# Plain float32 attention products, value products by column halves, and the softmax division moved onto the output

## The chip, the cores and the metric

The kernel runs on one core of a Trainium2 chip. The metric is the device time of one execution in microseconds (us). The times of the kernel before are 739.14, 739.26 and 741.04 us, so the median is 739.26. The execution that the profiler recorded took 739.67 us; its span, from the first to the last instruction, is 737.8 us.

## The reference

A sparse attention (2 batches, 8 heads, 768 positions, head size 64) feeds two feed-forward blocks. All arrays are float32 except the weights of the feed-forward blocks, which come as float64.

```python
scores = scale * np.matmul(q, k.transpose(0, 1, 3, 2))
keep = is_global | is_local          # first 8 keys, or the last 96 positions
scores = np.where(keep, scores + bias, -1e9)
a = np.exp(scores - max); a = a / (sum(a) + 1e-9)
x = np.matmul(a, v)                  # then heads side by side: 1536 x 512
h = x @ w_in;  x = (h * tanh(softplus(h))) @ w_out                 # 512 -> 2048 -> 512
g = x @ w_gate; out = ((silu(g) * (x @ w_val)) @ w_out2)           # 512 -> 1536 -> 512
```

## The kernel before

**Tiles and steps.** Of each batch the 768 positions are 6 tiles of 128 rows. A tile's attention is done in two steps, each for four heads (two pairs, p; a pair holds heads j = 0 and 1): 24 steps s. Since a row looks at the first 32 keys and at most 96 positions back, a step needs the key block of its own tile and one more block, that of the tile before, whose first 32 rows are replaced by the first 32 keys of the batch (`move_k` and `move_v`, GpSimd). The first tile of a batch has one block only (4 of the 24 steps).

**One step.** `transp` (L415) turns q and k with four products with the identity into PSUM. `qk` (L466) computes the scores of four heads: the two heads of a pair lie on partitions 0 to 63 and 64 to 127, so each product uses 64 rows of the array. `softmax` adds the bias and takes the minimum (VectorE, L483), takes the exponential with its sum (ScalarE, L311), and scales the rows by 1/sum (GpSimd, L496). `pv` turns the scaled rows (L515), copies them out of PSUM, and multiplies them with v (L535); a product yields both heads of a pair for 128 x 256, half of which is not used, and two copies (`xs`) take the two used quarters out. GpSimd then writes the result into `x`.

**Products in parts.** All products but the transposes are in float32r. Where more precision is wanted, each operand is kept in two parts: the operand as float32r, and the rest that this leaves. Three passes (`PASSES`) are added up: first by first, first by rest, rest by first. So q and k, the turned rows `et`, v, the weights and the hidden values are each copied once and subtracted once.

**Feed-forward work.** 68 weight units are fetched as float64 and made into float32 by ScalarE (L380) and four VectorE operations (L913 to L916), and then split. The first 12 units serve the "A products": the first six column blocks of the first feed-forward block, in 18 jobs for 256 tokens each (L349 with 256 columns, 432 products, and L738, 432 products), which are mixed in between the attention steps. Two jobs share a `mish` with two changes of the ScalarE table (L687, L689). All other products (512 columns, L349) come after the attention, since their weights use its space.

**Order.** All operations are first listed with costs and priorities, and a planner (`Plan.order`) plays them through with its own costs and writes each engine's queue in the order that comes out. Each engine then works through its queue in that order; copies can go to more than one engine, and the planner chooses. Buffers are handed out in the order in which they were listed. The transposes and the value products share a pool of two PSUM banks, `t_p`: a step takes four buffers of it, one for the next tile's q and k, two for the turned rows, and one (`o`) for the value products. 56 products of zeros (L575, 512 columns) keep TensorE busy: 6 at the start, and 50 of the lowest priority where the planner finds TensorE with nothing else to do.

Of the kernel before, what the change touches and what calls it, by code (L numbers as in the profile page):

```python
# [204 lines left out]
def kernel(  # L205
# [183 lines left out]
    raws, vts, scs, ebs = {}, {}, {}, {}  # L389
# [13 lines left out]

    def transp(i, hf):
# [12 lines left out]
        pv = lambda: ps.t.rearrange("p (a b s) -> p a b s", a=2, b=2)  # L417
        view = lambda a: kq.t[:, a, prs, c:3:2 - c, :]
        keys = lambda a: [(kq, (a, c, hf)), (kq, (a, 2, hf))]
        pe(emit, [(xk, hf), (xq, hf)], [(ps, 0)], 4, 256)  # L420
        copy(lambda: view(0), pv, [(ps, 0)], keys(0), psum_in=True, on="AV")
        arith(lambda: view(1), pv, lambda: view(0).bitcast(F32), ALU.subtract, [(ps, 0)] + keys(0), keys(1), on="V")

    def move_k(i, hf):
        b, t = tiles[i]
        if t == NT - 1:
            return
        prs = slice(2 * hf, 2 * hf + 2)
        own = lambda: kq.t[:, :, prs, t % 2, 0:WG]
        g = lambda: kg.t[:, :, prs, :]  # L430
        keys = [(kq, (a, t % 2, hf)) for a in range(2)]
        if t == 0:
            copy(g, lambda: own().bitcast(F32), keys, [(kg, hf)], n=128, on="G")
        else:
            copy(own, lambda: g().bitcast(F32), [(kg, hf)], keys, n=128, on="G")

    def split_v(i):
        x = raws["v", i]
        vt = vts[i] = plan.buf(vt_p)
        raw = lambda: x.t.rearrange("p h d -> p (h d)")  # L440
        copy(lambda: vt.t[:, 0], raw, [(x, 0), (x, 1)], [(vt, 0)], on="G")
        arith(lambda: vt.t[:, 1], raw, lambda: vt.t[:, 0].bitcast(F32), ALU.subtract, [(x, 0), (x, 1), (vt, 0)], [(vt, 1)],
              on="G")

    def move_v(i):
        b, t = tiles[i]
        vt = vts[i]
        V = [(vt, 0), (vt, 1)]
        if t == 0:
            copy(lambda: vg.t, lambda: vt.t[0:WG].bitcast(F32), V, [(vg, 0)], n=1024, on="G")  # L450
        elif t < NT - 1:
            copy(lambda: vt.t[0:WG], lambda: vg.t.bitcast(F32), [(vg, 0)], V, n=1024, on="G")

    def qk(s):
# [701 lines left out]
```

## Time and profile before

| what | us |
|---|---|
| median of three runs | 739.26 |
| profiled execution | 739.67 |
| its span | 737.8 |
| TensorE busy | 692.3 (94%) |
| VectorE busy | 445.6 (60%) |
| ScalarE busy | 373.1 (51%) |
| GpSimd busy | 324.2 (44%) |

The shares are means over two very different parts. In the profile, PE is TensorE's products and PEld its weight loads, DVE is VectorE, ACT is ScalarE, POOL is GpSimd, SP issues the DMAs. L numbers are lines of the kernel. A busy share of a stretch says how full an engine was; what ended its idle time stands in the view of waits.

### The profile page before, as it was taken

Reading aid. Unit: us, or ns where it says so; the run is one execution under the profiler, and the core shown is the slowest. Engines: PE = TensorE matmul, PEld = TensorE weight load, DVE = VectorE, ACT = ScalarE, POOL = GpSimd, SP = SyncE. Lnnn points to the kernel's source line nnn. Section 1 sums busy time; section 2 is a strip of 40 time slices with the busy share of each in tenths; the row PEclk is TensorE's granted clock in tenths of the full one; section 3 lists DMA queues with packets and bytes.
Section 4 is the critical chain, followed back from the end, with each engine's and each line's share of the span. In section 5 each row is a group of like instructions: output and inputs, shape, how many; then the busy total and the mean of one; then the engine's idle time right before and its main releaser. Section 6 shows DMA issues by size and latency. Waiting matters only on the chain.

```text
span 737.8 us, 10293 instructions
## 1 busy us (share of the span) xinstructions
PE 692.3 (94%) x3761; PEld 579.2 (79%) x3761; DVE 445.6 (60%) x843; ACT 373.1 (51%) x676; POOL 324.2 (44%) x378
## 2 busy tenths in 40 slices
PE   8958889889889999998999999999999999999996
PEld 6647779879889987766887877788878888888885
DVE  6998998764767685897688799711184111211312
ACT  5768677874767878766777843221232211111111
POOL 4887888666445332584276455211232111111111
PEclk9999999999999999999999999999999999999999
DMA  7634444230004442352323323410030210300301
GB/s 178 163 103 115 115 129 137 65 76 11 30 2 127 148 155 87 115 157 74 113 87 114 100 73 116 141 58 0 1 127 16 84 32 2 115 0 1 114 1 61
DMA packets 73161, 61.55 MB, mean 83 GB/s; under 512 B 39824, under 2 KB 63376, under 8 KB 73104
## 3 DMA queue, kind: packets, MB, share of 16 engines
q1 hardware_dynamic: 73104, 60.83, 27.9%
q8 instruction: 31, 0.51, 0.3%
q14 instruction: 26, 0.21, 0.1%
HBM read 51.38 MB, written 9.44 MB: 82 GB/s over the span
## 4 chain that ended last, share of the span: by engine, by line
PE 57%; DVE 26%; ACT 8%; issue 5%; DMA 2%; POOL 1%; SPq 0%; DVEq 0%; ACTq 0%; POOLq 0%
PE bank L349 47%; DVE cv L915 4%; PE bank L738 4%; DVE cv L916 3%; DVE cv L913 3%; DVE cv L914 2%; PE bank L535 2%; DVE a L340 2%; DVE et L521 2%; DVE e L483 2%; DVE g L340 2%; PE bank L515 1%; DVE kq L340 1%; ACT u L311 1%; ACT cv L380 1%
## 5 line engine op out<-in xcount | busy, mean ns | idle before, releaser
L349 PE MATMUL bank<-x,wa 128*128 128x512 f32 (+1 forms) x1008 | 193.3, 345 | 2.6 <-DVE a L340 1.1
L349 PEld LDWEIGHTS bank<-x,wa 128*128 128x128 f32 x1008 | 161.2, 189 | 27.3 <-DVE a L340 1.8
L340 POOL TENSOR_TENSOR g<-a,g 128x512 fp32r<-128x512 f32 x55 | 76.5, 1391 | 222.1 <-ACT g L332 221.5
L349 PE MATMUL bank<-x,wb 128*128 128x512 f32 x648 | 157.5, 396 | 0.2 <-DVE a L340 0.2
L349 PEld LDWEIGHTS bank<-x,wb 128*128 128x128 f32 x648 | 121.9, 188 | 29.8 <-DVE a L340 0.7
L332 ACT ACTIVATE g<-a 128x512 fp32r<-128x512 f32 x64 | 40.2, 632 | 134.1 <-DVE a L708 115.1
L311 ACT ACTIVATE u<-bank 128x512 f32<-128x512 f32 x84 | 49.7, 592 | 89.4 <-PE bank L349 89.3
L706 DVE SCALAR_TENSOR_TENSOR a<-u,bank 128x512 f32<-128x512 f32 x36 | 24.7, 686 | 112.6 <-ACT u L311 112.6
L349 PE MATMUL bank<-g,wb 128*128 128x512 f32 x288 | 72.5, 403 | 4.2 <-DVE g L340 2.1
L349 PE MATMUL bank<-wa,g 128*128 128x512 f32 x288 | 70.9, 392 | 2.3 <-DVE sb L567 1.7
L349 PEld LDWEIGHTS bank<-g,wb 128*128 128x128 f32 x288 | 54.5, 191 | 19.7 <-DVE g L340 3.3
L708 DVE TENSOR_TENSOR a<-a,bank 128x512 f32<-128x512 f32 x36 | 24.7, 687 | 68.4 <-PE bank L349 68.3
L349 PEld LDWEIGHTS bank<-wa,g 128*128 128x128 f32 x288 | 53.6, 188 | 15.8 <-DVE sb L567 2.4
L496 POOL TENSOR_SCALAR e<-e,sm 128x256 f32<-128x256 f32 (+1 forms) x96 | 56.5, 603 | 15.3 <-DVE sm L492 13.5
L915 DVE SCALAR_TENSOR_TENSOR cv<-raw,cv 128x512 int32<-128x512 int32 x68 | 61.3, 904 | 1.2
L913 DVE TENSOR_SCALAR cv<-cv 128x512 f32<-128x512 f32 x68 | 39.2, 579 | 35.9 <-ACT cv L380 35.7
L916 DVE SCALAR_TENSOR_TENSOR cv<-raw,cv 128x512 int32<-128x512 int32 x68 | 59.2, 873 | 1.1
L535 PE MATMUL bank<-et,vt 128*128 128x256 f32 x264 | 45.2, 304 | 14.1 <-DVE et L521 13.9
L311 ACT ACTIVATE e<-e,mn 128x256 f32<-128x256 f32 (+1 forms) x96 | 46.2, 483 | 19.6 <-DVE mn L483 19.5
L738 PE MATMUL bank<-g,wa 128*128 128x256 f32 x432 | 55.6, 284 | 0.5 <-DVE g L340 0.5
L380 ACT ACTIVATE cv<-raw 128x512 f32<-128x512 f32 x68 | 44.8, 666 | 20.7 <-DMA raw<-in_moe_w_gate_dram 6.6
L738 PEld LDWEIGHTS bank<-g,wa 128*128 128x128 f32 x432 | 53.2, 191 | 0.8 <-DVE g L340 0.7
(103 smaller groups left out, 984.6 us busy)
## 6 DMA issues: line engine op xcount, KB each, us to landing
raw<-in_moe_w_out_dram SPq DMA_DIRECT2D x28, 512.0 KB, 3.4
raw<-in_moe_w_in_dram SPq DMA_DIRECT2D x16, 512.0 KB, 3.9
raw<-in_moe_w_gate_dram SPq DMA_DIRECT2D x12, 512.0 KB, 3.6
raw<-in_moe_w_val_dram SPq DMA_DIRECT2D x12, 512.0 KB, 3.6
part<-st SPq DMA_DIRECT2D x16, 256.0 KB, 2.4
sb<-part SPq DMA_DIRECT2D x12, 256.0 KB, 3.0
st<-part SPq DMA_DIRECT2D x12, 256.0 KB, 3.0
in_q<-in_q_dram SPq DMA_DIRECT2D x11, 256.0 KB, 3.2
```

The source lines that it names most:

```text
L311: nc.scalar.activation(out=o(), in_=i(), func=func, scale=scale, **args)
L332: lambda: nc.scalar.activation(out=o(), in_=i(), func=AF.Copy, scale=scale)),
L340: return lambda: eng.tensor_tensor(out=o(), in0=x(), in1=y(), op=alu)
L349: nc.tensor.matmul(out=o, lhsT=lhs(a), rhs=rhs(b), start=first and i == 0, stop=last and i == len(PASSES) - 1)
L380: op([("A", 520, lambda: nc.scalar.activation(out=wf(), in_=hi().bitcast(F32), func=AF.Abs))], R, W_)
L496: op([("G", 160 + 0.836 * n, lambda x=x, f=f: nc.gpsimd.tensor_scalar(out=x(), in0=x(), scalar1=f(), scalar2=1.0, op0=ALU.mult, op1=ALU.mu ...
L535: nc.tensor.matmul(out=o.t[:, p * 256:(p + 1) * 256], lhsT=vt.t[:, a, pr * P:(pr + 1) * P], rhs=et2[p].t[:, x, c].rearrange("p j s -> p (j ...
L706: dve(lambda: nc.vector.scalar_tensor_tensor(out=a.t, in0=u.t[:, 0], scalar=1.0, in1=hg.t, op0=ALU.add, op1=ALU.mult), U + [(hg, 0)], A_)
L738: nc.tensor.matmul(out=y.t[:, dl * SUB:(dl + 1) * SUB], lhsT=ws[fl].t[:, a, d * P:(d + 1) * P], rhs=g.t[:, b, fl * SUB:(fl + 1) * SUB], st ...
L913: lambda: ts(out=f(), in0=f(), scalar1=F64_LOW, scalar2=F64_HIGH, op0=ALU.max, op1=ALU.min),
L915: lambda: stt(out=w(), in0=high(), scalar=-0x40000000, in1=w(), op0=ALU.bitwise_and, op1=ALU.bitwise_or),
L916: lambda: stt(out=w(), in0=low(), scalar=29, in1=w(), op0=ALU.logical_shift_right, op1=ALU.bitwise_or),
```

## The change

The attention is computed in plain float32, with no parts: `kq`, `et` and v lose their second half, and with it the subtractions. A score or value product is one plain float32 product where three float32r passes stood. Value products are done per head: 64 columns of weights (that head's v), written to PSUM partitions 0 to 63 or 64 to 127, 128 columns each, so nothing unused is computed. The rows are no longer scaled by GpSimd: 1/sum of each head is spread over 64 partitions by a product of it (broadcast) with the identity, into the unused half of the bank `o`; it is copied out (`rs`) and multiplied into the output by one VectorE operation, which takes the place of the two `xs` copies. The block before is no longer patched by GpSimd but fetched a second time into a pool `u`, in two DMAs (32 and 96 rows). The products of zeros read another buffer.

```diff
-    kq = fixed(asb, [P, 2, NP, 3, P], F32R, "kq")
+    kq = fixed(asb, [P, NP, 3, P], F32, "kq")
-    raw_in = {n: Pool(slots(asb, 1 if n == "v" else 2, [P, H, D], F32, "in_" + n)) for n in "qkv"}
-    vt_p = Pool(slots(asb, 3, [P, 2, H * D], F32R, "vt"))
+    raw_in = {n: Pool(slots(asb, 2, [P, H, D], F32, "in_" + n)) for n in "qkvu"}
-    xs_p = Pool(slots(asb, 1, [P, 2, P], F32, "xs"))
-    et_p = Pool(slots(asb, 2, [P, 2, 2, 2, P], F32R, "et"))
+    xs_p = Pool(slots(asb, 2, [P, 2, P], F32, "xs"))
+    rs_p = Pool(slots(asb, 2, [P, 2 * P], F32, "rs"))
+    et_p = Pool(slots(asb, 2, [P, 2, 2, P], F32, "et"))
...
+    def load_previous(i):
+        b, t = tiles[i]
+        if t == 0:
+            raws["u", i] = raws["v", i]
+        elif t < NT - 1:
+            x = raws["u", i] = plan.buf(raw_in["u"])
+            for ks, k0, hk in ((slice(0, WG), 0, 0), (slice(WG, P), t * P + WG, 1)):
+                dma(lambda ks=ks, k0=k0: nc.sync.dma_start(
+                    out=x.t[ks], in_=v[b, :, k0:k0 + ks.stop - ks.start, :].rearrange("h s d -> s h d")), [],
+                    [(x, hk)], kb=2 * (ks.stop - ks.start))
...
-        arith(lambda: view(1), pv, lambda: view(0).bitcast(F32), ALU.subtract, [(ps, 0)] + keys(0), keys(1), on="V")
...
-                for n, (a, c) in enumerate(PASSES):
-                    for j in range(2):
-                        ro = slice(64 * j, 64 * j + 64)
-                        nc.tensor.matmul(out=banks[j].t[:, p * 256:p * 256 + nb * P], lhsT=kq.t[ro, a, pr, 2, :],
-                                         rhs=kq.t[ro, c, pr, 0:nb, :].rearrange("p b s -> p (b s)"), start=n == 0, stop=n == len(PASSES) - 1)
-        pe(emit, [(kq, (a, c, hf)) for a in range(2) for c in (2, 0, 1)[:nb + 1]], [(banks[0], 0), (banks[1], 0)], 12, 256)
+                for j in range(2):
+                    ro = slice(64 * j, 64 * j + 64)
+                    nc.tensor.matmul(out=banks[j].t[:, p * 256:p * 256 + nb * P], lhsT=kq.t[ro, pr, 2, :],
+                                     rhs=kq.t[ro, pr, 0:nb, :].rearrange("p b s -> p (b s)"), start=True, stop=True)
+        pe(emit, [(kq, (c, hf)) for c in (2, 0, 1)[:nb + 1]], [(banks[0], 0), (banks[1], 0)], 8, 256)
...
-            op([("G", 160 + 0.836 * n, lambda x=x, f=f: nc.gpsimd.tensor_scalar(
-                out=x(), in0=x(), scalar1=f(), scalar2=1.0, op0=ALU.mult, op1=ALU.mult))], [(sm, u)], [(e, u)])
...
-            dve(lambda et=et, pv4=pv4: nc.vector.tensor_tensor(
-                out=et.t[:, 1, 0:nb], in0=pv4()[:, 0:nb], in1=et.t[:, 0, 0:nb].bitcast(F32), op=ALU.subtract),
-                [(ps, 0), (et, 0)], [(et, 1)], n=n)
...
+        def over():
+            for u in range(4):
+                p, j = divmod(u, 2)
+                nc.tensor.matmul(out=o.t[64 * j:64 * j + 64, (2 + p) * P:(3 + p) * P],
+                                 lhsT=sm.t[:, u:u + 1].to_broadcast([P, D]), rhs=ident, start=True, stop=True)
+        pe(over, [(sm, u) for u in range(4)], [(o, 2)], 4, 256)
+        rs = plan.buf(rs_p)
+        copy(lambda: rs.t, lambda: o.t[:, 2 * P:4 * P], [(o, 2)], [(rs, 0)], n=256, psum_in=True, on="AV")
...
-                    for a, x in PASSES:
-                        nc.tensor.matmul(out=o.t[:, p * 256:(p + 1) * 256], lhsT=vt.t[:, a, pr * P:(pr + 1) * P],
-                                         rhs=et2[p].t[:, x, c].rearrange("p j s -> p (j s)"),
-                                         start=n == 0, stop=n == 3 * len(blks) - 1)
+                    for j in range(2):
+                        nc.tensor.matmul(out=o.t[64 * j:64 * j + 64, p * P:(p + 1) * P],
+                                         lhsT=v_of(c).t[:, 4 * hf + 2 * p + j, :], rhs=et2[p].t[:, c, j, :],
+                                         start=c == 0, stop=c == nb - 1)
...
-            copy(lambda ro=ro: xs.t[ro], lambda ro=ro, j=j: o4()[ro, :, j, :], [(o, 0), (o, 1)], [(xs, j)],
-                 psum_in=True, n=256, on="AV")
+        dve(lambda: nc.vector.tensor_tensor(out=xs.t.rearrange("p a s -> p (a s)"), in0=o.t[:, 0:2 * P],
+                                            in1=rs.t, op=ALU.mult), [(o, 0), (o, 1), (rs, 0)], [(xs, 0)],
+            n=256)
...
-                split_v(i)
+                load_previous(i)
...
-            if hh == 1:
-                move_v(ii)
```

Since the planner's operations and costs are others, every engine's queue is others too. Three places matter below.

First, TensorE in the middle of the attention, in the kernel before: the end of a step's scores (`kq`), then transposes of rows (`e`), value products (`vt`) and transposes of q and k.

```order
L466 MATMUL bank_102<-kq 128x256
L466 MATMUL bank_103<-kq 128x256
L515 MATMUL bank_104<-ident,e_129 128x128 x4
L535 MATMUL bank_105<-et_136,vt_124 128x256 x3
L535 MATMUL bank_105<-et_136,vt_125 128x256 x3
L535 MATMUL bank_105<-et_135,vt_124 128x256 x3
L535 MATMUL bank_105<-et_135,vt_125 128x256 x3
```

The same place in the changed kernel: value products of one step (L522), scores (L455), transposes (L499), a block of A products (L348) and the products that spread 1/sum (L511, from `sm`).

```order
L522 MATMUL bank_104<-et_137,in_v_122 64x128 x2
L522 MATMUL bank_104<-et_137,in_u_124 64x128 x2
L522 MATMUL bank_104<-et_138,in_v_122 64x128 x2
L522 MATMUL bank_104<-et_138,in_u_124 64x128 x2
L455 MATMUL bank_102<-kq 128x256
L455 MATMUL bank_103<-kq 128x256
L455 MATMUL bank_102<-kq 128x256
L455 MATMUL bank_103<-kq 128x256
L499 MATMUL bank_105<-ident,e_127 128x128 x4
L499 MATMUL bank_104<-ident,e_127 128x128 x4
L348 MATMUL bank_106<-x_73,wa_76 128x256 x12
L511 MATMUL bank_105<-ident,sm_130 64x128 x4
```

A step's 12 score products became 4, its 12 value products of 128 x 256 became 8 of 64 x 128, and 4 products for 1/sum came in, in a place of their own, ahead of the value products.

Second, VectorE in the second step of the kernel before, where the first weight unit (`cv`) comes in.

```order
L340 TENSOR_TENSOR kq<-bank_105,kq 128x2x2x128
L340 TENSOR_TENSOR kq<-bank_104,kq 128x2x256
L491 TENSOR_SCALAR sm_130<-sm_130 128x4
L492 RECIPROCAL sm_130<-sm_130 128x4
L913 TENSOR_SCALAR cv_91<-cv_91 128x512
L914 TENSOR_SCALAR cv_91<-cv_91 128x512
```

The first weight unit on VectorE in the changed kernel, which comes in the fifth step; `rs` is the spread 1/sum, L531 the multiplication.

```order
L328 TENSOR_SCALAR rs_136<-bank_104 128x256
L328 TENSOR_SCALAR kq<-bank_105 128x2x2x128
L531 TENSOR_TENSOR xs_134<-bank_104,rs_136 128x256
L480 TENSOR_SCALAR sm_132<-sm_132 128x4
L481 RECIPROCAL sm_132<-sm_132 128x4
L894 TENSOR_SCALAR cv_91<-cv_91 128x512
```

Weight units begin three steps later; in both kernels 16 of the 68 stand ahead of the end of the last step's bias work.

Third, TensorE at the end of the attention before: the last value products, the one transpose of the check of the arguments (L651), and A products behind them.

```order
L535 MATMUL bank_104<-et_135,vt_125 128x256 x3
L535 MATMUL bank_104<-et_135,vt_126 128x256 x3
L651 MATMUL bank_105<-ident,chk 1x128
L349 MATMUL bank_106<-x_75,wa_76 128x256 x12
L349 MATMUL bank_107<-x_75,wa_80 128x256 x12
```

And in the changed kernel:

```order
L522 MATMUL bank_104<-et_138,in_u_125 64x128 x2
L522 MATMUL bank_104<-et_138,in_v_123 64x128 x2
L635 MATMUL bank_105<-ident,chk 1x128
L348 MATMUL bank_104<-x_74,wa_80 128x256 x12
L348 MATMUL bank_105<-x_74,wa_84 128x256 x12
L348 MATMUL bank_104<-x_74,wa_82 128x256 x12
```

Of the 864 A products, 336 stand behind the last value products before, and 432 in the changed kernel. The 56 products of zeros, all ahead of the seventh step's scores before, are spread over the whole attention.

## Rows read from the trace of the kernel before

**Rows 1.** The profile's page: span, and engines' busy time with share and count.
```profile
span 737.8 us, 10293 instructions
PE 692.3 (94%) x3761; PEld 579.2 (79%) x3761; DVE 445.6 (60%) x843; ACT 373.1 (51%) x676; POOL 324.2 (44%) x378
```

**Rows 2.** Busy us by stretch (from:to length, engines with instructions, clock, DMA share).
```profile
0.00:120.00 120.00, 97.96 (x710) 83.63 (x711) 108.34 (x287) 84.70 (x224) 94.81 (x145) 0.97 0.50 127
120.00:212.00 92.00, 83.14 (x700) 76.91 (x700) 60.96 (x171) 62.84 (x142) 55.35 (x90) 1.00 0.22 59
212.00:260.00 48.00, 48.00 (x372) 46.58 (x370) 34.57 (x53) 35.66 (x46) 22.67 (x21) 1.00 0.37 117
260.00:738.00 478.00, 463.21 (x1985) 372.07 (x1983) 241.71 (x335) 189.89 (x267) 151.35 (x123) 0.99 0.23 74
```

**Rows 3.** Chain of waits, 0 to 120 us: shares by line, and its first transfer.
```profile
by line: DVE e L483 9.4%; DVE et L521 8.6%; DVE cv L916 8.2%; DVE cv L915 8.0%; issue 6.5%; DVE kq L340 5.3%; DVE cv L913 4.7%; DVE sm L491 4.5%; DVE wa L340 4.3%; PE bank L466 4.0%; PE bank L575 3.9%; PE bank L415 3.6%; ACT e L311 3.6%; PE
...
2.13 3.67 DMA in_k<-in_k_dram
```

**Rows 4.** Waits of TensorE, 0 to 212 us (waiter <- releaser: us, times, longest).
```profile
PE bank L535 <- DVE et L521: 13.9, 14, 2.3
PE bank L515 <- ACT xs L332: 4.9, 5, 1.9
PE bank L515 <- DVE xs L329: 2.3, 3, 1.2
```

**Rows 5.** Timeline of TensorE (start, us until its last end, what, count).
```profile
18.06 0.98 PE L466 MATMUL bank<-kq 64*128 64x256 f32 x12
18.96 0.44 PE L515 MATMUL bank<-ident,e 128*128 128x128 f32 x2
...
19.61 1.55 PE L575 MATMUL bank<-et 128*128 128x512 f32 x6
21.00 0.62 PE L535 MATMUL bank<-et,vt 128*128 128x256 f32 x3
21.46 0.28 PE L415 MATMUL bank<-ident,in_k 128*128 128x128 f32 x1
21.57 0.27 PE L415 MATMUL bank<-ident,in_q 128*128 128x128 f32 x1
...
211.32 0.86 PE L535 MATMUL bank<-et,vt 128*128 128x256 f32 x5 [0.34 <-DVE et L521]
...
230.84 5.32 PE L738 MATMUL bank<-g,wa 128*128 128x256 f32 x43
```

**Rows 6.** VectorE's groups by shape (count | busy us, mean ns | idle before).
```profile
L340 DVE TENSOR_TENSOR a<-bank,u 128x512 f32<-128x512 f32 x48 | 31.4, 683 | 8.9 <-ACT u L311 8.8
L521 DVE TENSOR_TENSOR et<-bank,et 128x512 fp32r<-128x512 f32 x40 | 26.7, 681 | 19.4 <-ACT et L332 19.3
L340 DVE TENSOR_TENSOR kq<-bank,kq 128x512 fp32r<-128x512 f32 x24 | 16.2, 680 | 3.5 <-ACT kq L332 3.3
L329 DVE TENSOR_SCALAR xs<-bank 64x256 f32<-64x256 f32 x11 | 4.6, 420 | 2.5 <-PE bank L535 2.4
L521 DVE TENSOR_TENSOR et<-bank,et 128x256 fp32r<-128x256 f32 x8 | 3.2, 415 | 0.1
```

**Rows 7.** ScalarE's groups by shape.
```profile
L311 ACT ACTIVATE u<-bank 128x512 f32<-128x512 f32 x84 | 49.7, 592 | 89.4 <-PE bank L349 89.3
L687 ACT ACT_TABLE_LOAD x24 | 30.8, 1283 | 0.4
L688 ACT ACTIVATE u<-u 128x1024 f32<-128x1024 f32 x24 | 25.5, 1061 | 0.3
L332 ACT ACTIVATE xs<-bank 64x256 f32<-64x256 f32 x37 | 14.0, 377 | 8.2 <-PE bank L535 7.0 <-DVE xs L329 0.7
L332 ACT ACTIVATE et<-bank 128x256 fp32r<-128x256 f32 x8 | 2.9, 381 | 1.1 <-PE bank L515 1.0 <-PE bank L535 0.2
```

**Rows 8.** GpSimd's groups by shape.
```profile
L496 POOL TENSOR_SCALAR e<-e,sm 128x256 f32<-128x256 f32 (+1 forms) x96 | 56.5, 603 | 15.3 <-DVE sm L492 13.5
```

More of the change, by code (lines that the diff above doesn't have):

```diff
@@ L388 @@
     NTL = len(tiles)
-    raws, vts, scs, ebs = {}, {}, {}, {}
+    raws, scs, ebs, sms = {}, {}, {}, {}
     def load(i, names="qk"):
@@ L415, in emit @@
                 nc.tensor.transpose(ps.t[:, p * P:(p + 1) * P], x.t[:, h:h + 2, :].rearrange("s h d -> s (h d)"), ident)
-        pv = lambda: ps.t.rearrange("p (a b s) -> p a b s", a=2, b=2)
-        view = lambda a: kq.t[:, a, prs, c:3:2 - c, :]
-        keys = lambda a: [(kq, (a, c, hf)), (kq, (a, 2, hf))]
         pe(emit, [(xk, hf), (xq, hf)], [(ps, 0)], 4, 256)
-        copy(lambda: view(0), pv, [(ps, 0)], keys(0), psum_in=True, on="AV")
-        arith(lambda: view(1), pv, lambda: view(0).bitcast(F32), ALU.subtract, [(ps, 0)] + keys(0), keys(1), on="V")
+        copy(lambda: kq.t[:, prs, c:3:2 - c, :], lambda: ps.t.rearrange("p (a b s) -> p a b s", a=2, b=2), [(ps, 0)],
+             [(kq, (c, hf)), (kq, (2, hf))], psum_in=True, on="AV")
     def move_k(i, hf):
@@ L428, in move_k @@
         prs = slice(2 * hf, 2 * hf + 2)
-        own = lambda: kq.t[:, :, prs, t % 2, 0:WG]
-        g = lambda: kg.t[:, :, prs, :]
-        keys = [(kq, (a, t % 2, hf)) for a in range(2)]
+        own = lambda: kq.t[:, prs, t % 2, 0:WG]
+        g = lambda: kg.t[:, prs, :]
         if t == 0:
-            copy(g, lambda: own().bitcast(F32), keys, [(kg, hf)], n=128, on="G")
+            copy(g, own, [(kq, (t % 2, hf))], [(kg, hf)], n=64, on="G")
         else:
[L435 to L452, printed above, removed]
+            copy(own, g, [(kg, hf)], [(kq, (t % 2, hf))], n=64, on="G")
     def qk(s):
@@ L476, in softmax @@
         e = ebs[s] = plan.buf(e_p)
-        sm = plan.buf(sm_p)
+        sm = sms[s] = plan.buf(sm_p)
         m = lambda u: mn.t[:, s * 4 + u:s * 4 + u + 1]
@@ L492, in softmax @@
         dve(lambda: nc.vector.reciprocal(out=sm.t, in_=sm.t), S4, S4, n=30)
-        for u in range(4):
-            x = lambda u=u: e.t[:, u, 0:n]
-            f = lambda u=u: sm.t[:, u:u + 1]
-            op([("G", 160 + 0.836 * n, lambda x=x, f=f: nc.gpsimd.tensor_scalar(
-                out=x(), in0=x(), scalar1=f(), scalar2=1.0, op0=ALU.mult, op1=ALU.mult))], [(sm, u)], [(e, u)])
     def pv(s):
@@ L501, in pv @@
         b, t = tiles[i]
-        e = ebs.pop(s)
+        e, sm = ebs.pop(s), sms.pop(s)
         blks = (0,) if t == 0 else (0, 1)
         nb = len(blks)
-        v_of = lambda c: vts[i if c == t % 2 else i - 1]
+        v_of = lambda c: raws["v", i] if c == t % 2 else raws["u", i - 1]
         et2 = []
@@ L544, in pv @@
         xs = plan.buf(xs_p)
-        for j in range(2):
-            ro = slice(64 * j, 64 * j + 64)
-            copy(lambda ro=ro: xs.t[ro], lambda ro=ro, j=j: o4()[ro, :, j, :], [(o, 0), (o, 1)], [(xs, j)],
-                 psum_in=True, n=256, on="AV")
+        dve(lambda: nc.vector.tensor_tensor(out=xs.t.rearrange("p a s -> p (a s)"), in0=o.t[:, 0:2 * P],
+                                            in1=rs.t, op=ALU.mult), [(o, 0), (o, 1), (rs, 0)], [(xs, 0)],
+            n=256)
         dst = lambda a: x.t[:, a, 2 * hf:2 * hf + 2, o0:o0 + P]
         ks = lambda a: [(x, (a, 2 * hf + p, o0 // P)) for p in range(2)]
-        XS = [(xs, 0), (xs, 1)]
-        copy(lambda: dst(0), lambda: xs.t, XS, ks(0), n=256, on="G")
-        arith(lambda: dst(1), lambda: xs.t, lambda: dst(0).bitcast(F32), ALU.subtract, XS + ks(0), ks(1), n=256,
+        copy(lambda: dst(0), lambda: xs.t, [(xs, 0)], ks(0), n=256, on="G")
+        arith(lambda: dst(1), lambda: xs.t, lambda: dst(0).bitcast(F32), ALU.subtract, [(xs, 0)] + ks(0), ks(1), n=256,
               on="G")
```

24 lines of the change are left out of this document (8 added, 16 removed).

## The prediction

> **What bounds the kernel now.** I read the page first: TensorE is busy for 94% of the span, the others for 44 to 60% [rows 1]. Then the stretches, since the mean hides two programs [rows 2]. From 212 us on TensorE is all but full (511 of 526 us): what happens there is the time of its products. Up to 120 us VectorE is the fullest engine (108.3 of 120 us, TensorE 98.0). The chain of waits up to 120 us confirms it [rows 3]: mostly VectorE, with the two operations that the change deletes in it, the subtraction for the rest of the rows (L521) at 8.6% and that of q and k (L340 on `kq`) at 5.3%. TensorE's waits up to 212 us say the same from its side [rows 4]: 13.9 us for L521, 7.2 us for the `xs` copies, which also go. So the attention stretch is bound by VectorE and ScalarE together, and the change takes work from them and gives work to TensorE. The question is whether TensorE has room for it.
>
> TensorE's room, from the timeline [rows 5]. The unit costs: a plain float32 transpose of 128 columns starts 0.11 us after the one before (21.46 to 21.57); a float32r product of 256 columns takes 0.12 (43 in 5.3 us); one of 512, 0.23 (six zero products between 19.61 and 21.00); the 12 score products of a step 0.90 (18.06 to 18.96). Two score products on the two halves of the rows run at the same time: 12 x 0.12 would be 1.44. Six pairs at 0.12 are 0.72, so 0.18 of the 0.90 goes into entering and leaving the split array. Over the attention stretch: 272 transposes at 0.11 are 29.9 us, 264 value products at 0.12 31.7, 24 steps of scores 21.6, 56 zero products 12.9, and the 528 A products ahead of the last value product (864 less 336) 63.4. The sum is 159.5 of 212 us. The first keys land only at 5.8 us [rows 3], so 46.5 us are left in which TensorE waits or is late.
>
> **The change part by part.**
>
> VectorE and ScalarE lose the rests, 26.7 + 3.2 us for the rows and 16.2 for q and k, and the `xs` copies, 4.6 + 14.0: 64.7 us [rows 6, 7]. They gain a copy of 128 x 256 out of PSUM per step (nearest row: 0.38 us on ScalarE [rows 7]) and a multiplication of that size (0.415 on VectorE [rows 6]): 24 x 0.80 = 19.1. In the new order 96 A products more stand behind the attention; they are two jobs with one `mish`: two reads of PSUM, two table changes and two long passes on ScalarE, 2 x 0.59 + 2 x 1.28 + 2 x 1.06 = 5.9 us [rows 7], and some 2.7 us on VectorE (two products at 0.68 [rows 6] and as much again for splitting). So of the 316.8 us that both engines are busy up to 212 us [rows 2], 262.6 are left.
>
> GpSimd loses the scaling of the rows, 56.5 us [rows 8], and the splitting and patching of v. It is not the fullest engine anywhere, but the scaling stands between 1/sum and the transposes, so each step also gets 4 x 0.60 us shorter.
>
> TensorE: no plain float32 product stands in this trace, only transposes. From below, such a product costs what one float32r pass costs, 0.06 us per 128 columns; from above, four passes, 0.24. The nearest row is the plain float32 transpose, 0.11 per 128 columns, about twice float32r: there one operand is an identity, which is exact in one part. A product has two full operands, so I take twice that, 0.22 per 128 columns, as two passes of 0.11, one after the other on their part of the array. The Trainium skill states four passes for true float32 (FP8 and Floating Point Precision, TensorE Precision Notes); by that the price would be the upper end, 0.24, and the sum would be 5 us longer.
>
> Whether two halves of the array still overlap is the second unknown. Rows on 64 and 64 partitions do with float32r [rows 5]; halves by columns do not occur in the trace. Bounds: full overlap, and none. I take overlap for both, since the nearest row shows it, but in the order written: both passes of one head, then both of the other, so that a pass can only start beside the second pass of its neighbour. Then n products take n + 1 slots of one pass and not 2n. To each group in halves I add the 0.18 from above.
> - Scores, 20 steps with two blocks: 5 slots of 0.22 + 0.18 = 1.28 instead of 0.90, together +7.6 us. The 4 steps with one block come out within 0.2 us of before.
> - Value products: 9 slots of 0.11 + 0.18 = 1.17 instead of 12 x 0.12 = 1.44, together -5.4.
> - Spreading 1/sum: new, 5 x 0.11 + 0.18 = 0.73, 24 times, +17.5.
> Together +19.7 us on TensorE. The Trainium skill gives the reason for the 0.18, and it speaks against the change: changing the tiling mode drains TensorE (TensorEngine Tiling (Array Packing), Key Properties). The change adds two such groups per step.
>
> Fetching the block before twice costs 16 DMAs on SP's queue. The DMA engines are busy for 50% up to 120 us and 22% after [rows 2], and weight units begin three steps later in the new order; I take nothing. If SP's queue stands at such a fetch because its buffer is still in use, weight fetches behind it come late; that would be about one landing per case, 3.7 us as for the first keys [rows 3], with A products that wait for the unit.
>
> **The sum.** Attention stretch after: 159.5 + 19.7 - 96 x 0.12 (the A products that move behind) = 167.6, and 6 at the start, so TensorE can't end it before 173.6 us. Of the 46.5 us of waiting I keep 15: of about 31 us that TensorE stands still up to 212 us (212 less 181.1 busy [rows 2]), 21.1 are for operations that go [rows 4], so a third stays (one multiplication takes the place of the two `xs` copies, on an engine that is no longer full). That is 188.6. VectorE and ScalarE then have 262.6 us of work in 2 x 188.6, 70% full, against 75% before and 80% up to 120 us: no longer the bound, though near it. What is late next is TensorE itself. The last value product ended at 212.2 [rows 5], 525.6 us before the end; to these come the 11.5 us of A products: 537.1. Span 725.7; the profiled execution has 1.9 us around its span, so 727.6, taken as 728. That execution is 0.4 us above the median, which changes nothing.
>
> **Rivals.**
>
> 1. The column halves do not overlap. For it: no row shows them overlapping. Against it: the row halves do. Value products then take 16 x 0.11 + 0.18 = 1.94 (+11 us with the one-block steps instead of -5.4), 1/sum 8 x 0.11 + 0.18 = 1.06 (25.4 instead of 17.5): 24.7 us more than in the forecast. TensorE needs 198 us; being fuller, it keeps only 10 of waiting: 208, a span of 745, 747 us. It decides as soon as TensorE's added work is more than the waiting that goes, 31.5 us (the A products that move shorten one stretch and lengthen the other). The Trainium skill is against this rival: it reports column packing as concurrent, 2.38 times faster for three tiles (TensorE: Matmul & The Clock Gate, Part 3); no run here shows it.
> 2. Plain float32 products overlap in no half. Scores 8 x 0.22 + 0.18 = 1.94, 14 us more: TensorE needs 212, with 10 of waiting 222, 761 us.
> 3. The waiting is not given back. `over` takes the bank `o` before the value products and holds it until the multiplication; the pool has two banks, so the next tile's transposes wait longer. Price: the 0.73 of the new group and about 0.2 for its hand-over, 24 times, 22 us, of which A products cover some 9: 728 + 13 = 741. For it: TensorE's waits on L515 for `xs` [rows 4] are waits for such a bank. Against it: the `et` copies and the scaling, which lengthened the same loop, are gone.
> 4. A plain product costs a single pass. Then 1/sum and value products are nearly free, TensorE's sum is some 25 us below before, and VectorE and ScalarE are the bound at 80%: 164 us and 6 at the start, 170 + 537 + 2 = 709.
>
> **Chances.** Forecast 0.50 (its own range 717 to 738, from 4 to 25 us of waiting kept), rival 1 0.22, rival 2 0.10, rival 3 0.13, rival 4 0.05. The range 714 to 757 leaves out most of rivals 2 and 4. A change of 0.3% (2.2 us) is about what can be told from none: faster takes 0.47 of the forecast, 0.04 of rival 3 and rival 4: 0.56; the same 0.02, 0.06 and 0.01 of rival 1: 0.09; slower the rest, 0.35.
>
> **What will show it.** In the changed profile: score groups (L455) of four take 1.1 to 1.3 us if row halves overlap, 1.8 to 2.0 if not; four products of 1/sum (L511) 0.55 to 0.75 or 0.9 to 1.1; eight value products (L522) 1.0 to 1.2 or 1.8 to 2.0. VectorE up to 120 us should fall well below 90%. The last value product should end near 189 us; near 208, rival 1. If L499 waits long for `xs` or `rs`, rival 3. The forecast is wrong if TensorE's groups cost more than 1.5 times these numbers, or if the stretch behind the last value product is not 537 us, since nothing in my sum touches it but the A products.

## The result, and the profile after

| | before | changed |
|---|---|---|
| median, us | 739.2 (4 runs, 738.67 to 741.04) | 719.52 (4 runs, 719.23 to 719.93) |
| profiled execution / its span, us | as above | 719.93 / 718.2 |
| last value product ends, us | 212.2 | 182.9 |
| from there to the end of the span, us | 525.6 | 535.3 |

The ratio is 0.9727 (95% interval 0.971 to 0.9743): the change makes the kernel 19.7 us faster. The forecast was 728 us, in a range of 714 to 757.

The span and the busy times on the profile's page of the changed kernel; they answer to [rows 1].

```profile
span 718.2 us, 10474 instructions
PE 692.5 (96%) x3945; PEld 566.8 (79%) x3945; DVE 400.7 (56%) x797; ACT 358.6 (50%) x648; POOL 238.6 (33%) x250
```

VectorE, ScalarE and GpSimd all have less work; TensorE has as many busy microseconds as before, in a shorter span. By stretch, with the columns of [rows 2] (the attention now ends at 183, not at 212):

```profile
0.00:120.00 120.00, 111.06 (x948) 83.21 (x948) 96.91 (x323) 87.81 (x249) 51.09 (x88) 1.00 0.68 159
120.00:183.00 63.00, 61.22 (x549) 53.97 (x549) 24.93 (x77) 33.37 (x76) 17.36 (x24) 1.00 0.18 51
```

Up to 120 us TensorE went from 97.96 to 111.06 us busy, VectorE from 108.34 to 96.91. From 120 us to the end of the attention TensorE is busy for 61.2 of 63 us. The granted clock there is at 1.00, where the mean of the first 120 us was 0.97 before.

The chain of waits of the changed kernel, 0 to 120 us, as shares by line; it answers to [rows 3]:

```profile
by line: PE bank L455 13.7%; PE bank L499 11.5%; PE bank L522 10.9%; PE bank L348 10.4%; PE bank L559 9.2%; PE bank L426 9.0%; PE bank L511 7.3%; DVE cv L894 3.2%; issue 3.1%; DMA in_k<-in_k_dram 3.0%; DVE cv L896 2.8%; DVE e L472 2.4%; DVE
```

The first seven entries are TensorE: scores, transposes, value products, A products, zeros, q and k, and the new spreading of 1/sum (L511). Before, VectorE's lines led. TensorE's longest waits up to 183 us, in the columns of [rows 4]:

```profile
PE bank L522 <- DVE rs L328: 2.2, 4, 0.6
PE bank L522 <- ACT rs L331: 1.9, 4, 0.5
PE bank L559 <- DVE g L556: 1.5, 1, 1.5
PE bank L426 <- DMA in_k<-in_k_dram: 1.0, 1, 1.0
PE bank L499 <- DVE xs L531: 0.9, 1, 0.9
```

The 13.9 us on the subtractions are gone, and of the 7.2 us on the `xs` copies 0.9 are left. What is new is small: 4.1 us in which the value products wait for the copy `rs` (L328 on VectorE, L331 on ScalarE), though by the kernel they only share the bank that it reads.

TensorE's timeline in the middle of the attention (start, us until its last end, what, count; a plain float32 product leaves two records, so x8 at L455 is four products):

```profile
59.92 0.66 PE L511 MATMUL bank<-ident,sm 128*64 128x128 f32 x8
60.51 0.33 PE L426 MATMUL bank<-ident,in_k 128*128 128x128 f32 x1
...
62.99 0.66 PE L499 MATMUL bank<-ident,e 128*128 128x128 f32 x4 [0.80 <-DVE kq L328]
63.58 1.13 PE L455 MATMUL bank<-kq 64*128 64x256 f32 x8
64.64 0.55 PE L499 MATMUL bank<-ident,e 128*128 128x128 f32 x3
...
181.83 0.44 PE L522 MATMUL bank<-et,in_u 128*64 128x128 f32 x4
182.10 0.39 PE L522 MATMUL bank<-et,in_v 128*64 128x128 f32 x4
182.31 0.39 PE L522 MATMUL bank<-et,in_u 128*64 128x128 f32 x4
182.53 0.39 PE L522 MATMUL bank<-et,in_v 128*64 128x128 f32 x4
182.85 0.27 PE L635 MATMUL bank<-ident,chk 128*1 128x128 f32 x1
```

From the start of a group to the start of the next: spread 0.59 us, scores 1.06, eight value products 1.02. All three are cheaper than forecast (0.73, 1.28, 1.17).

### The profile page after: what moved, and what is told of

It reads as the page before. It is cut to its first block, busy times and chain, and to the rows that moved or that the text cites. A ratio compares the mean times of both kernels' runs of the same rounds, so it can differ in the third digit from the quotient of the medians.

```text
span 718.2 us, 10474 instructions
## 1 busy us (share of the span) xinstructions
PE 692.5 (96%) x3945; PEld 566.8 (79%) x3945; DVE 400.7 (56%) x797; ACT 358.6 (50%) x648; POOL 238.6 (33%) x250
## 4 chain that ended last, share of the span: by engine, by line
PE 66%; DVE 16%; ACT 9%; issue 5%; DMA 2%; POOL 1%; SPq 0%; DVEq 0%; ACTq 0%; POOLq 0%
PE bank L348 48%; PE bank L722 5%; DVE cv L894 3%; PE bank L455 3%; DVE cv L896 3%; DVE cv L897 3%; PE bank L499 3%; PE bank L522 2%; ACT L671 2%; DVE cv L895 2%; DVE a L339 2%; PE bank L426 2%; PE bank L559 2%; ACT u L672 2%; PE bank L511 2%
## 5 line engine op out<-in xcount | busy, mean ns | idle before, releaser
L348 PE MATMUL bank<-x,wa 128*128 128x512 f32 (+1 forms) x1008 | 192.3, 345 | 1.5 <-POOL wa L339 0.6
L348 PEld LDWEIGHTS bank<-x,wa 128*128 128x128 f32 x1008 | 161.4, 189 | 26.6 <-issue 1.0
L339 POOL TENSOR_TENSOR g<-a,g 128x512 fp32r<-128x512 f32 x60 | 84.4, 1407 | 231.2 <-ACT g L331 229.5
L348 PE MATMUL bank<-x,wb 128*128 128x512 f32 x648 | 157.2, 395 | 1.3 <-DVE a L339 1.3
L348 PEld LDWEIGHTS bank<-x,wb 128*128 128x128 f32 x648 | 121.6, 188 | 30.7 <-DVE a L339 1.8
L331 ACT ACTIVATE g<-a 128x512 fp32r<-128x512 f32 x66 | 41.2, 631 | 131.7 <-DVE a L692 114.9
L348 PE MATMUL bank<-wa,g 128*128 128x512 f32 x288 | 70.9, 392 | 2.2 <-DVE st L551 1.8
L348 PE MATMUL bank<-g,wb 128*128 128x512 f32 x288 | 70.2, 397 | 2.4 <-POOL g L339 1.6
L348 PEld LDWEIGHTS bank<-g,wb 128*128 128x128 f32 x288 | 53.9, 188 | 16.7 <-POOL g L339 2.5
L348 PEld LDWEIGHTS bank<-wa,g 128*128 128x128 f32 x288 | 53.6, 188 | 15.8 <-DVE st L551 2.5
L897 DVE SCALAR_TENSOR_TENSOR cv<-raw,cv 128x512 int32<-128x512 int32 x68 | 57.6, 848 | 1.0
L896 DVE SCALAR_TENSOR_TENSOR cv<-raw,cv 128x512 int32<-128x512 int32 x68 | 57.3, 845 | 1.2
L339 POOL TENSOR_TENSOR wa<-cv,wa 128x512 fp32r<-128x512 f32 x27 | 35.4, 1310 | 54.0 <-ACT wa L331 51.9
L339 POOL TENSOR_TENSOR wb<-cv,wb 128x512 fp32r<-128x512 f32 x27 | 37.5, 1389 | 29.1 <-ACT wb L331 27.9
```

The lines of the kernel that those rows point to most:

```text
L331: lambda: nc.scalar.activation(out=o(), in_=i(), func=AF.Copy, scale=scale)),
L339: return lambda: eng.tensor_tensor(out=o(), in0=x(), in1=y(), op=alu)
L348: nc.tensor.matmul(out=o, lhsT=lhs(a), rhs=rhs(b), start=first and i == 0, stop=last and i == len(PASSES) - 1)
L896: lambda: stt(out=w(), in0=high(), scalar=-0x40000000, in1=w(), op0=ALU.bitwise_and, op1=ALU.bitwise_or),
L897: lambda: stt(out=w(), in0=low(), scalar=29, in1=w(), op0=ALU.logical_shift_right, op1=ALU.bitwise_or),
```

## The experiments

Theory A is the prediction's: the attention waits for VectorE and ScalarE; what is taken from them shortens it until TensorE is the bound. Theory B puts the gain on GpSimd: the scaling of the rows, which stood between 1/sum and the transposes, is gone. Theory C: TensorE's own products became cheaper. In the table "T" is the end of the last value product in the profiled execution; medians stand beside runs of the kernel before on the same chip.

| run | kernel | median, us | ratio to before (95%) | T, us |
|---|---|---|---|---|
| e1_scores | before + scores plain | 731.22 | 0.9899 (0.9859 to 0.9939) | 208.8 |
| e2_values | before + values plain | 725.38 | 0.9804 (0.9761 to 0.9848) | 195.2 |
| e3_nospread | changed, GpSimd scales rows | 712.42 | 0.964 (0.9605 to 0.9675) | 184.4 |
| e4_order | changed, halves one after the other | 720.68 | 0.975 (0.9714 to 0.9786) | 183.9 |
| e5_nozero | changed, 50 zero products out | 719.55 | 0.9709 (0.9677 to 0.9741) | 191.1 |
| e6_dvework | changed + 72 idle operations on VectorE | 731.72 | 0.9871 (0.9839 to 0.9903) | 204.4 |
| e7_merge | changed, spread joined to a value group | 726.93 | 0.9806 (0.9775 to 0.9837) | 183.4 |
| e8_plainzero | changed, zero products plain float32 | 726.48, one run | none | 176.3 |
| e9_double | changed, spread issued twice | 729.33 | 0.985 (0.9823 to 0.9878) | 191.6 |
| e10_nospread_nozero | e3 + e5 | 714.68 | 0.966 (0.9634 to 0.9686) | 184.8 |
| e11_changed | changed, again | 719.17 | 0.9711 (0.9687 to 0.9735) | 183.5 |

**Which part pays.** e1 takes the kernel before and makes only the scores plain.

```diff
-    kq = fixed(asb, [P, 2, NP, 3, P], F32R, "kq")
+    kq = fixed(asb, [P, NP, 3, P], F32, "kq")
...
-        arith(lambda: view(1), pv, lambda: view(0).bitcast(F32), ALU.subtract, [(ps, 0)] + keys(0), keys(1), on="V")
...
-                for n, (a, c) in enumerate(PASSES):
+                    nc.tensor.matmul(out=banks[j].t[:, p * 256:p * 256 + nb * P], lhsT=kq.t[ro, pr, 2, :],
```

> The kernel before with one part of the change alone: scores in plain float32 (q and k without rests). Theory A (VectorE and ScalarE bounded the attention, and taking their work away made the time): 24 subtractions of 0.68 us go (16.2 us), TensorE gets 20 x 0.16 = 3 us more; about half of 16 comes out: 731 us (727 to 735). Rival B (the scaling by GpSimd between 1/sum and the transposes was what each step waited for): scaling stays, so 739 (736 to 743). Rival C (TensorE's own products became cheaper): 742, the 3 us more.

Measured: 731.22, 7.6 us below before, as theory A had it. Theory C fails for this part: TensorE's score groups became dearer (1.06 us instead of 0.90), and the kernel faster. The wait on the other subtraction, which e1 keeps, is still TensorE's longest up to 212 us in e1:

```profile
PE bank L530 <- DVE et L516: 9.5, 14, 1.6
```

e2 makes only the value products plain, by column halves, and fetches the block before twice; GpSimd still scales the rows, and nothing is spread.

```diff
-    et_p = Pool(slots(asb, 2, [P, 2, 2, 2, P], F32R, "et"))
+    et_p = Pool(slots(asb, 2, [P, 2, 2, P], F32, "et"))
...
-                    for a, x in PASSES:
+                    for j in range(2):
+                        nc.tensor.matmul(out=o.t[64 * j:64 * j + 64, p * P:(p + 1) * P],
+                                         lhsT=v_of(c).t[:, 4 * hf + 2 * p + j, :], rhs=et2[p].t[:, c, j, :],
...
-        for j in range(2):
+        copy(lambda: xs.t.rearrange("p a s -> p (a s)"), lambda: o.t[:, 0:2 * P], [(o, 0), (o, 1)], [(xs, 0)],
...
```

> The kernel before with another part alone: value products in plain float32 by column halves, v fetched twice, one copy of the output instead of two; rows are still scaled by GpSimd, scores still in three passes. Theory A: VectorE and ScalarE lose 29.9 us of subtractions and half of the 18.6 us of output copies, TensorE 20 x 0.45 = 9: 721 us (715 to 728). Rival B: little, 734 (730 to 739), since the scaling stays. Rival C: 730, the 9 us of TensorE.

Measured: 725.38, 13.4 us below before, in theory A's range; theory C's 730 lies outside the interval (721 to 728 us). But e2 does not part A from C as e1 does: TensorE's value products also became cheaper here, by what e2 expected to be 9 us. e3 does both, and leaves out only the spreading: GpSimd's scaling and one `xs` copy come back.

```diff
+            op([("G", 160 + 0.836 * n, lambda x=x, f=f: nc.gpsimd.tensor_scalar(
+                out=x(), in0=x(), scalar1=f(), scalar2=1.0, op0=ALU.mult, op1=ALU.mult))], [(sm, u)], [(e, u)])
...
-        pe(over, [(sm, u) for u in range(4)], [(o, 2)], 4, 256)
-        copy(lambda: rs.t, lambda: o.t[:, 2 * P:4 * P], [(o, 2)], [(rs, 0)], n=256, psum_in=True, on="AV")
...
-        dve(lambda: nc.vector.tensor_tensor(out=xs.t.rearrange("p a s -> p (a s)"), in0=o.t[:, 0:2 * P],
+        copy(lambda: xs.t.rearrange("p a s -> p (a s)"), lambda: o.t[:, 0:2 * P], [(o, 0), (o, 1)], [(xs, 0)],
...
```

> The changed kernel without the spreading of 1/sum: GpSimd scales the rows as before, the output is copied once per step. TensorE loses 24 groups of 0.43 us and as many changes of the array's division (together 12 to 17 us), GpSimd gets 56 us back. Theory A (the changed kernel's attention is bound by TensorE): faster than the changed kernel, 710 (705 to 716). Rival B: the scaling was the wait that went, so slower than it, 726 (722 to 735). Rival C: 708.

Measured: 712.42, the fastest of all kernels here; its interval (0.9605 to 0.9675) does not touch that of the changed kernel, run again as e11 (0.9687 to 0.9735). That ends theory B: GpSimd has the scaling again, and the kernel is 7 us faster, not slower. The first stretch of e3:

```profile
0.00:120.00 120.00, 111.42 (x855) 85.50 (x856) 92.29 (x289) 88.53 (x247) 90.08 (x155) 1.00 0.68 163
```

GpSimd is at 90.1 us where the changed kernel has 51.1, and TensorE is as full in both. T is 184.4 in e3, later than the 182.9 of the changed kernel, but 336 A products stand behind it instead of 432: e3 has done some 96 more by then, worth 11.5 us, and gains 10 at an equal count (182.9 + 11.5 - 184.4).

**Who is the bound now.** e9 issues each spread product twice. The planner sees the same operation, so all queues keep their order; of the other edits only that of e4 is as clean in this respect.

```diff
-            for u in range(4):
+            for u in (0, 1, 2, 3, 0, 1, 2, 3):
```

> The changed kernel with the four products that spread 1/sum issued twice in place (all queues in the same order). If TensorE is the bound of the attention (theory A): each of the 24 groups is 0.43 us longer, 10.5 us, and most of it comes out: 727 to 730. If TensorE has waiting to spare at these places, and the spread costs by its place in the order or by the bank it holds (rival): at most 3 us more, 720 to 723.

A group in e9, and what follows it, in the timeline's columns:

```profile
62.95 1.09 PE L511 MATMUL bank<-ident,sm 128*64 128x128 f32 x16
63.98 0.33 PE L426 MATMUL bank<-ident,in_k 128*128 128x128 f32 x1
```

A group takes 1.03 us instead of 0.59, 24 times: 10.6 us more on TensorE. The median is 10.2 us above e11, the span of the profiled execution 8.2 (726.0 and 717.8), T 8.1. Added work on TensorE appears in the time for the most part: TensorE is the bound of the attention. e6 puts a load like the old one back on VectorE, in 72 subtractions of a buffer that nobody reads, so no one waits for their result.

```diff
+        dve(lambda: nc.vector.tensor_tensor(out=dump.t, in0=dump2.t, in1=dump2.t, op=ALU.subtract), [(dump2, 0)], [(dump, k)],
+            n=512)
...
+        spare(1)
...
+            spare(2)
```

> The changed kernel with VectorE work put back that nothing waits for: per step one subtraction of 128 x 512 for q and k and two for the rows, into a buffer that is not read (72 in all, some 0.7 to 0.9 us each, 50 to 65 us). Theory A (VectorE's work was the bound, so the relief made the gain): most of the gain goes, 735 us (729 to 742). Rival B (the shorter chain of each step made it): little, 720 to 725, since no step waits for these.

The added operations of e6 (duration in ns: least, median, most; first and last start), then its first stretch and TensorE's two longest waits up to 204 us:

```profile
L417 DVE TENSOR_TENSOR dump<-dump x72: 652/691/1657, 2.4 to 141.5; 128x512 f32<-128x512 f32 x72
...
0.00:120.00 120.00, 108.29 (x885) 84.17 (x886) 117.89 (x312) 86.22 (x231) 67.42 (x89) 0.99 0.63 148
...
PE bank L505 <- DVE xs L538: 4.3, 4, 1.7
PE bank L461 <- DVE mn L478: 3.3, 2, 2.0
```

VectorE is busy for 117.9 of 120 us, more than before the change, and 12.2 us of the gain are gone (731.72 against 719.52; 10.7 by the ratios to before), with work on no chain at all. TensorE waits for VectorE again, for `xs` (0.9 us in the changed kernel) and for `mn`. That is theory A from its other side: load on VectorE sets back the attention. The size is not all VectorE's own. GpSimd's operations became dearer beside the added ones (its copies into `x` 0.81 us instead of 0.50 on average up to 142 us), and TensorE's granted clock was at 0.50 (1.2 GHz instead of 2.4) for three stretches of 3.4 us, two of them up to T; that is worth half of their time at most, 5.1 us.

**How the halves overlap.** The forecast had the two passes of a plain product start in the order of the queue. e4 writes all products of one half ahead of those of the other.

```diff
-            for p in range(2):
-                for j in range(2):
+            for j in range(2):
+                for p in range(2):
...
-            for u in range(4):
+            for u in (0, 2, 1, 3):
...
-                for c in blks:
-                    for j in range(2):
+                for j in range(2):
+                    for c in blks:
```

> The changed kernel with products of one half of the array written one after the other (both products of head 0's half, then both of head 1's), instead of alternating; nothing else. If halves overlap only where neighbours in the queue are on different halves: scores take 7 to 8 slots of 0.216 instead of 4, value products 14 to 16 of 0.109 instead of 8, spreading 7 to 8 instead of 4, some 35 to 47 us more on TensorE: 750 to 764. If a product's own two passes are what runs side by side and the halves never overlapped, or if the engine looks far enough ahead in its queue: within 2 us of the changed kernel, 718 to 722.

Groups of e4 on TensorE's timeline (the last is a whole step's value products):

```profile
60.39 0.66 PE L511 MATMUL bank<-ident,sm 128*64 128x128 f32 x8
60.98 0.33 PE L426 MATMUL bank<-ident,in_k 128*128 128x128 f32 x1
...
61.57 0.53 PE L522 MATMUL bank<-et,in_v 128*64 128x128 f32 x4
61.84 0.48 PE L522 MATMUL bank<-et,in_u 128*64 128x128 f32 x4
...
64.04 1.14 PE L455 MATMUL bank<-kq 64*128 64x256 f32 x8
65.11 0.66 PE L499 MATMUL bank<-ident,e 128*128 128x128 f32 x4
...
182.77 0.45 PE L522 MATMUL bank<-et,in_u 128*64 128x128 f32 x4
...
183.85 0.27 PE L635 MATMUL bank<-ident,chk 128*1 128x128 f32 x1
```

Spread 0.59 and scores 1.07: as with the halves alternating. The eight value products take 1.08 (182.77 to 183.85) instead of 1.02. As the kernel writes them for e4, a product from `in_u` for the first half stands ahead of the one from `in_v` for the second half. In the trace both `in_v` products (four records) start before any `in_u`: the second half starts ahead of what is written before it. So the order hardly matters for the overlap: 0.06 us a step, 1.2 us in 20 steps, and e4's time, 720.68, is 1.2 us above that of the changed kernel (no run of one lies within the runs of the other). The Trainium skill says otherwise: matmuls start and end in program order, a strict FIFO (TensorE: Matmul & The Clock Gate, Part 3); here the measurement decides, as far as the queue is in the order that the kernel writes, which no view shows.

e8 prices the plain product on the whole array: the zero products become plain float32, 128 x 128.

```diff
...
-            nc.tensor.matmul(out=ps.t, lhsT=t()[:, 0:P], rhs=t()[:, 0:512], start=True, stop=True)
+            nc.tensor.matmul(out=ps.t[:, 0:P], lhsT=t()[:, 0:P], rhs=t()[:, 0:P], start=True, stop=True)
```

> The changed kernel with its products of zeros in plain float32 on the whole array, 128 columns instead of 512 in float32r: measures a plain product by itself. If a plain product is two passes at half rate (the estimate of the prediction): 0.22 us from one to the next, so 8 value products in 8 slots of 0.109 mean that halves overlap in full. If it is one such pass: 0.11, and the halves do not overlap. If four passes of 0.06: 0.24. The time stays within 2 us of the changed kernel.

```profile
13.44 1.06 PE L559 MATMUL bank<-u 128*128 128x128 f32 x8
14.34 0.38 PE L499 MATMUL bank<-ident,e 128*128 128x128 f32 x2
```

In e8's timeline four products with eight records take 0.90 us: 0.113 a record, 0.225 a product. Eight value products, sixteen records, take 1.02 us; in a row on the whole array they would take 1.80. The price, 0.225, lies between the 0.22 of two passes of 0.11 and the 0.24 of four passes of 0.06 and doesn't part them; a product leaves two records. What e8 expected of the time was missed: the planner's order became another one (528 A products behind T instead of 432), so its 726.48 says nothing on the price.

**Two tries for more, both without gain.** e5 leaves out 50 of the 56 zero products, e10 does so in e3.

```diff
-    LATE = 50
+    LATE = 0
```

> The changed kernel without the 50 products of zeros of lowest priority (the 6 at the start stay). Theory A (TensorE is the bound of the attention now): they are 50 x 0.23 = 11.5 us of TensorE's queue, and 6 to 11 us come off: 711 us (708 to 714). Rival: the planner put them where TensorE waits anyway, so nothing comes off: 718 to 721; or TensorE's granted clock falls in the early steps without them: over 721.

> The changed kernel without the spreading (rows scaled by GpSimd) and without the 50 zero products of lowest priority. Theory A: with 12.9 us of zeros in a full TensorE queue, some of them come off: 706 (702 to 710). Rival: as in the changed kernel, they only fill waiting that stays: 710 to 713 like without the spreading alone.

e5's first stretch:

```profile
0.00:120.00 120.00, 106.35 (x912) 84.70 (x914) 92.05 (x296) 87.49 (x234) 50.15 (x84) 0.99 0.64 157
```

719.55 and 714.68: no gain on the changed kernel, none on e3 (712.42). TensorE is 4.7 us less busy up to 120 us in e5 and waits in their place. Its granted clock also fell, which e5's expectation had as its last case; the stretch, in the same columns:

```profile
77.40:80.80 3.40, 3.40 (x19) 3.40 (x18) 3.40 (x10) 0.91 (x4) 1.56 (x2) 0.50 0.00 0
```

The clock was at 0.50 (1.2 GHz) for 3.4 us, after TensorE had stood idle for 1.13 and 0.99 us shortly before; in e10 it was there twice up to 120 us, for 6.8 and 3.4 us. In the changed kernel and in e3 it does not fall before the last product. So these stretches took back at most 1.7 us of what e5 saved, and 5.1 in e10. The order changed too: in e5 336 A products stand behind T, so at an equal count its attention is 3.3 us shorter (182.9 + 11.5 - 191.1), which the stretch behind it loses. That the zero products cost nothing by themselves is not shown.

e7 puts the spread products into one group with the value products of the first pair, to enter the split array once less per step.

```diff
-        pe(over, [(sm, u) for u in range(4)], [(o, 2)], 4, 256)
...
+                if p == 0:
+                    over()
...
-            pe(emit, [(v_of(c), hk) for c in blks for hk in range(2)] + [(et2[p], 0)], [(o, p)], 4 * len(blks), 256)
+            pe(emit, [(v_of(c), hk) for c in blks for hk in range(2)] + [(et2[p], 0)] + [(sm, u) for u in range(4) if p == 0],
+               [(o, p)] + [(o, 2)] * (p == 0), 4 * len(blks) + 4 * (p == 0), 256)
...
```

> The changed kernel with the products that spread 1/sum put into one group with the value products, so the array changes its division once per step instead of twice. Theory A: TensorE saves some 0.2 to 0.3 us a step, 5 to 7 us: 714 us (711 to 717). Rival: the copy of the spread 1/sum now comes after the value products' start and the bank is held longer, so the saving is lost: 718 to 723.

The timeline of e7 around one such group:

```profile
61.81 0.66 PE L511 MATMUL bank<-ident,sm 128*64 128x128 f32 x8
62.30 0.39 PE L522 MATMUL bank<-et,in_v 128*64 128x128 f32 x4
62.52 0.39 PE L522 MATMUL bank<-et,in_u 128*64 128x128 f32 x4
62.84 0.33 PE L426 MATMUL bank<-ident,in_k 128*128 128x128 f32 x1
...
63.43 0.44 PE L522 MATMUL bank<-et,in_v 128*64 128x128 f32 x4
```

Joined to value products the spread takes 0.49 us instead of 0.59 (61.81 to 62.30). But the planner put transposes of q and k between the two pairs, so a step still enters the split array twice here, and T is 183.4, nothing saved. The 7 us are lost behind the attention (541.7 us, 535.3 in the changed kernel). Between 183 and 300 us, first TensorE's longest wait in e7 and a stretch of its clock, then the wait in the changed kernel:

```profile
PE bank L348 <- DVE a L339: 6.5, 3, 3.1
276.40:283.20 6.80, 5.91 (x14) 4.67 (x15) 4.73 (x6) 5.39 (x7) 6.41 (x5) 0.50 0.49 155
```

```profile
PE bank L348 <- DVE a L339: 1.3, 1, 1.3
```

Products there wait for VectorE's `a`, 5.2 us more than in the changed kernel, and within the longest of these waits (3.1 us) the granted clock fell to 0.50 for 6.8 us, which costs at most 3 us more. The edit didn't touch these products, only their place among the others.

## Why the prediction was right, and where its sum was not

**What bounds, and what decides: right.** VectorE and ScalarE held the attention, and less work for them shortened it (e1, e2, e6). VectorE fell to 81% up to 120 us, "well below 90%"; together the two have 243.0 us of work up to 183 us, where 262.6 were forecast. What is late next is TensorE itself: the chain shows it, and e9 confirms it.

**TensorE's added work: too high by 10.7 us.** The step that failed is "a pass can only start beside the second pass of its neighbour. Then n products take n + 1 slots". The halves overlap in full, nearly whatever the order (e4), so n products take n slots of a pass.

| | forecast | measured |
|---|---|---|
| scores, 20 groups | 1.28, +7.6 | 1.06, +3.2 (0.16 x 20) |
| value products, 20 groups | 1.17, -5.4 | 1.02, -8.4 (0.42 x 20) |
| spread, 24 groups | 0.73, +17.5 | 0.59, +14.2 |
| together | +19.7 | +9.0 |

The two other parts of the price held. A plain product costs two times 0.11 per 128 columns, as taken from the transposes (e8: 0.225 in all, forecast 0.22; four passes of 0.06 would be 0.24, not far off). Entering and leaving the split array costs 0.14 to 0.18: scores 1.06 less four slots of 0.22, values 1.02 less eight of 0.11, spread 0.59 less four of 0.11. In e7, where value products follow at once, the spread takes 0.49.

**"Of the 46.5 us of waiting I keep 15": too low by 4.9.** Measured are 182.9 - (159.5 + 9.0 - 11.5) - 6 = 19.9 us. The mistake can be seen in before's own windows: of the 46.5 only 24.9 were idle time (212 - 181.1 - 6), the other 21.6 were busy time above the unit costs (181.1 - 159.5), from products that don't follow one another at full rate. The idle part fell by 20.2, close to the 21.1 that the list of waits gave: TensorE stands still for 10.7 of 183 us now, 6 of them at the start. The busy part only fell to 15.3 (172.3 - 157.0). Some of that fall comes from the granted clock, which was no step of the prediction. Two stretches of before, with what TensorE did just ahead of them and in the first:

```profile
68.19 0.76 PE L515 MATMUL bank<-ident,e 128*128 128x128 f32 x4 [1.87 <-ACT xs L332]
68.88 1.65 PE L466 MATMUL bank<-kq 64*128 64x256 f32 x12
70.46 1.11 PE L515 MATMUL bank<-ident,e 128*128 128x128 f32 x4
106.17 1.62 PE L535 MATMUL bank<-et,vt 128*128 128x256 f32 x6 [2.29 <-DVE et L521]
...
68.60:72.00 3.40, 3.40 (x22) 2.90 (x21) 2.21 (x5) 3.36 (x4) 3.40 (x7) 0.50 0.92 243
106.20:109.60 3.40, 3.40 (x16) 3.40 (x16) 2.56 (x11) 3.37 (x3) 3.32 (x5) 0.50 0.59 133
```

TensorE stood idle for 1.87 and 2.29 us, then the clock was at 0.50 (1.2 GHz) for 3.4 us each time, with TensorE full; the twelve score products in the first took 1.58 us instead of 0.90. That costs 3.4 us at most. In the changed kernel, where TensorE's longest wait up to 183 us is 1.5 us, the clock does not fall before TensorE is done. A third such stretch of before, at 341.7 us, lies behind the attention. So at most 5.1 of the 19.7 us came by way of these stretches. The first products run slowly in both kernels (transposes 0.21 us apart), until 9.3 us in the changed kernel and beyond 12 us in the kernel before; TensorE also waits for transfers there, and what this is worth was not separated.

**Behind the attention: 535.3 instead of 537.1**, 1.9 us less. In the runs whose A products were counted, this stretch less 0.12 us for each moves by some 4 us either way whenever an edit gives the planner another list, so nothing is read from 1.9; before's third stretch at half the clock, 1.7 us at most, is of the same size.

The sum: -10.7 + 4.9 - 1.9 = -7.7, from 727.6 to 719.9.

**The rivals.** 1 and 2 are out: both kinds of halves overlap. 3 is out: transposes wait 0.9 us for `xs`, with 22 us feared. 4 is out as a price (0.225, not the 0.06 of one pass). But the spread does cost something, in another place than rival 3 had it: not by a held bank, but by its 14.2 us on TensorE, which the relief of GpSimd doesn't repay (e3). The forecast asked of each edit only what it costs within the whole; had it asked what the spread buys alone, [rows 2] said that GpSimd was not the fullest engine, and the answer would have been: little. The second fetch of v came out at nothing, as taken: TensorE has no wait on `in_u`, though SP's queue stood at this fetch for 7.0 us in all.

**By part, from the runs:** scores -7.6 us, value products -13.4, both together -26.4 (712.42 beside 738.79), spreading +7. That both give 5.4 more than their sum stays open. It fits one bound that each part alone only half removes, but the planner's order differs in all three, and so does the clock: in the profiled executions it was at 0.50 for 3.4 us three times in before, twice in e1, four times in e2, and in e3 not before TensorE was done. That is worth some microseconds either way; its part was not separated.

## What to carry to other kernels

Where one engine bounds a stretch and the next has idle time there, price each part of a change on both engines by itself: here two parts paid 26 us and the third gave 7 back, because it relieved an engine that nobody waited for and loaded the one that came next. Split a ledger's remainder into idle time, which a removed wait gives back, and busy time above the unit costs, most of which it does not. Read the granted clock beside the waits: here waits of 2 to 3 us came with 3.4 to 6.8 us at half the clock (before, e7). And where a planner orders the work, test a cost by an edit that it can't see (e4, e9): most others move the rest by some microseconds as well.

## What the runs showed of the hardware

- A plain float32 product leaves two records of 0.11 us per 128 columns each, the price of two plain transposes (0.225 for 128 x 128 in e8).
- Products on two column halves, 64 columns of weights each, run at the same time: sixteen records in 1.02 us. The halves share the time in full when they alternate, and nearly so when the kernel writes them one after the other (1.08, e4).
- Going into split products and back cost 0.14 to 0.18 us a group; a spread group that value products follow directly is 0.10 shorter (e7). The Trainium skill states that a change of the tiling mode drains TensorE (TensorEngine Tiling (Array Packing), Key Properties); the groups agree.
- With waits of TensorE of 1.87, 2.29 (before) and 3.1 us (e7) came a granted clock of 0.50 (1.2 GHz) for 3.4, 3.4 and 6.8 us; it fell just after the first two and within the third. In the changed kernel, whose longest wait up to 183 us is 1.5 us, it did not fall before the last product.
